# Sums and value products in separate PSUM tiles, output rows by DMAs of 32 partitions, batch edges in the mask, and the second tile's products within the first FFN

## The chip, the cores and the metric

The kernel runs on one core of one Trainium2 chip. The metric is device microseconds of that core, the median of several executions.

## The reference

Sliding-window causal attention (window 64) over 8 batches of 576 rows and 8 heads of 64, followed by a SwiGLU FFN over the 4608 rows that come out:

```
scores = (q @ k^T) / 8, masked to 0 <= i - j < 64
attn   = exp(scores) / sum(exp(scores)) @ v          # 8 x 8 x 576 x 64
x      = attn as 4608 x 512
out    = (silu(x @ w_gate) * (x @ w_val)) @ w_out     # d_ff = 1536, fp32 out
```

## The kernel before

The 4608 rows are cut into 9 tiles of 512 ("tile" in this text means these 512 rows, or a buffer where "PSUM tile" is said). A tile has attention for four pairs of heads (`u`), then 12 FFN steps (`gate_value`, 8 matmuls of 128x512 each), then four output projections of 12 matmuls. From tile 2 on, the attention of a tile is laid between the projections of the tile before. The parts that matter:

```python
def sums(t, u, d_ps):                      # denominators, and their inverse on ScalarE
    for h in range(2):
        nc.tensor.matmul(d_ps[64 * h:64 * h + 64, :], ones[:], E[:, h, :])
    nc.scalar.activation(ld[:], d_ps[:], AF.Ln)
    nc.scalar.activation(r[:], ld[:], AF.Exp, scale=-1.0)

def values(t, u, o_ps):                    # 16 products with V, then the scaling
    ... nc.tensor.matmul(blocks(o_ps[64 * h:64 * h + 64], t, m, m + 1), v..., E...)
    nc.vector.tensor_mul(xT[t][:, u, :], o_ps[:], inverse.pop((t, u))[:])

def products(t, u):                        # tiles 2 to 8
    da = ps_a.tile([P, 2, 512], FP32, name="da_ps", tag="a")
    sums(t, u, da[:, 0])
    values(t, u, da[:, 1])

def project(t, s):                         # 12 matmuls, a copy, one output DMA
    ...
    rows = rows.rearrange("(r e) f -> e r f", e=16)[4 * s:4 * s + 4]   # tiles 2 to 8
    nc.sync.dma_start(rows, os_[:])

# the head (cut): tile 0's scores and sums; load tile 1's Q and K; cast V; load gate and value
# weights; load tile 1's V; shift V on VectorE and do tile 0's values; tile 1's scores and sums
front(0)
... cast_v(0); for s in range(4): weights_gv(384 * s, 384 * s + 384)
load_v(nc.gpsimd, v1[1], 1)
back(0)                                    # shift_v by VectorE, then values(0, 0..3)
front(1)
for m in range(12):
    gate_value(0, m)
back(1)                                    # shift_v by VectorE, then values(1, 0..3)
for m in range(12):
    gate_value(1, m) ...
```

`scores` sets a batch edge to zero in the weights `E` by two GpSimd memsets per head pair. `shift_v` builds a copy of V moved by 64 rows, because even and odd blocks of keys need V at different partitions.

The softmax here doesn't subtract the row's maximum and nothing guards it: scores larger than these inputs give would overflow.

## Time and profile before

| | before |
|---|---|
| median of 3 runs | 391.09 us (390.72 to 391.17) |
| span of the profiled run | 390.2 us |
| first FFN starts (its first weight load) | 39.9 us |
| scores of tile 2 | 89.6 us |
| a steady tile, FFN to FFN | 38.4 us |
| last matmul ends | 379.9 us |

In the profile, PE is TensorE (PEld its weight loads), DVE is VectorE, ACT is ScalarE, POOL is GpSimd and SP is SyncE; a q after the name marks the issuing of a DMA by that engine. PSUM is the memory that matmuls write. A "value group" is the 16 products with V of one head pair. The "head" of the kernel is all before the first FFN, its "tail" all after the last matmul. The profiled run of the kernel before took 391.94 us, 0.8 above the median.

In the timeline, a line holds a start, a duration, an engine, a source line of the kernel, an operation, what it writes and reads, and in brackets the idle time just before it and what ended it. The waits view holds, for an engine and line, what was waited for, the total in us, how often, and the longest.

### The profile page before, as it was taken

How to read it: one execution, taken by the hardware profiler on the slowest of the kernel's cores; microseconds unless marked ns; L12 is line 12 of the kernel's file. 1: busy time of each engine (PE TensorE's matmuls, PEld its weight loads, DVE VectorE, ACT ScalarE, POOL GpSimd, SP SyncE). 2: the span in 40 equal slices, each digit the busy share in tenths (PEclk: the TensorE clock that was granted, in tenths of full speed). 3: DMA queues.
4: the chain of work that ended last, by engine and by line, in shares of the span. 5: the costliest groups of instructions: out<-in, count | busy, mean ns of one | idle time of the engine just before them, and what ended most of it. 6: DMA issues, size and time to landing. Idle time of an engine off the chain costs nothing.

```text
span 390.2 us, 6851 instructions
## 1 busy us (share of the span) xinstructions
PE 333.9 (86%) x2670; PEld 159.3 (41%) x2712; DVE 217.9 (56%) x305; ACT 164.4 (42%) x236; POOL 144.5 (37%) x306
## 2 busy tenths in 40 slices
PE   3564996999889997998799979988998899889990
PEld 2353343444334443444344434444444344434440
DVE  4887246576335773577356736673666376633420
ACT  1636531335333366336533753374337434743300
POOL 6962894470076016551652255435423000000000
PEclk9995799899999999999999999999999999999997
DMA  8999899970489606990798079807961130110012
GB/s 266 167 195 182 127 116 174 183 72 35 135 167 231 119 6 126 181 159 9 129 196 142 12 138 187 134 21 144 188 118 28 57 81 2 31 54 25 2 42 66
DMA packets 76224, 43.35 MB, mean 111 GB/s; under 512 B 56928, under 2 KB 70688, under 8 KB 76192
## 3 DMA queue, kind: packets, MB, share of 16 engines
q0 software_dynamic: 38320, 20.37, 41.0%
q1 hardware_dynamic: 36784, 21.50, 21.1%
q10 hardware_dynamic: 1088, 1.05, 0.8%
q8 instruction: 21, 0.34, 0.4%
q14 instruction: 11, 0.09, 0.1%
HBM read 50.14 MB, written 9.44 MB: 153 GB/s over the span
## 4 chain that ended last, share of the span: by engine, by line
PE 80%; DMA 6%; ACT 4%; POOL 3%; issue 2%; DVE 2%; SPq 0%; DVEq 0%; POOLq 0%
PE v_ps L260 24%; PE g_ps L260 24%; PE o_ps L271 23%; ACT ld L230 4%; PE da_ps L241 3%; DMA wg<-in_moe_w_gate_dram 3%; PE da_ps L228 2%; PE s_ps L203 2%; DMA out_dram<-os__4362 2%; DMA q<-in_q_dram 2%; POOL v L139 1%; POOL q_n L79 1%; POOL k_n L79 1%; POOL wg L151 0%; POOL wv L151 0%
## 5 line engine op out<-in xcount | busy, mean ns | idle before, releaser
L265 ACT ACTIVATE sg<-g_ps 128x512 f32<-128x512 f32 x108 | 64.5, 597 | 134.4 <-PE g_ps L260 109.6
L266 DVE TENSOR_TENSOR hT<-sg,v_ps 128x512 bf16<-128x512 f32 x108 | 74.8, 693 | 74.9 <-PE v_ps L260 73.9
L260 PE MATMUL v_ps<-xT,wv 128*128 128x512 bf16 x426 | 112.0, 384 | 0.4
L260 PE MATMUL g_ps<-xT,wg 128*128 128x512 bf16 x420 | 110.9, 383 | 0.9 <-issue 0.6
L271 PE MATMUL o_ps<-wo,hT 128*128 128x512 bf16 x408 | 96.3, 380 | 1.7 <-issue 0.8
L110 POOL DMA_DIRECT2D k_s<-in_k_dram x124 | 66.3, 540 | 49.2 <-DMA q_s<-in_q_dram 32.7
L260 PEld LDWEIGHTS <-wv 128*128 128x128 bf16 x432 | 42.7, 99 | 52.2 <-issue 2.2
L260 PEld LDWEIGHTS <-wg 128*128 128x128 bf16 x432 | 42.6, 99 | 52.3 <-issue 2.8
L271 PEld LDWEIGHTS <-hT 128*128 128x128 bf16 x432 | 39.7, 98 | 45.1
L212 ACT ACTIVATE E<-s_ps 128x1024 bf16<-128x1024 f32 (+1 forms) x36 | 35.0, 1008 | 18.0 <-PE s_ps L203 17.9
L222 POOL MEMSET E<- 64x64 bf16 x56 | 6.5, 147 | 83.7 <-DVE E L213 83.7
L187 DVE STREAM_TRANSPOSE kT<-k_s 128x512 bf16<-128x512 bf16 x28 | 35.8, 1277 | 0.0
L246 DVE TENSOR_TENSOR xT<-da_ps,r 128x512 bf16<-128x512 f32 x28 | 19.4, 692 | 23.6 <-ACT r L232 13.6
L230 ACT ACTIVATE ld<-da_ps 128x512 f32<-128x512 f32 x28 | 16.7, 598 | 37.1 <-PE da_ps L228 36.0
L92 POOL DMA_DIRECT2D q_s<-in_q_dram x52 | 28.9, 566 | 3.3 <-DMA v<-in_v_dram 2.5
L241 PE MATMUL da_ps<-E,v 128*64 128x64 bf16 x448 | 12.4, 196 | 19.7 <-ACT ld L230 19.7
L241 PEld LDWEIGHTS <-v 128*64 128x64 bf16 x576 | 14.6, 116 | 33.2 <-issue 29.0
L213 DVE TENSOR_TENSOR E<-E,maskp 128x1024 bf16<-128x1024 bf16 x28 | 19.4, 693 | 12.9 <-ACT E L212 12.9
L232 ACT ACTIVATE r<-ld 128x512 f32<-128x512 f32 x36 | 22.7, 631 | 1.1
L203 PE MATMUL s_ps<-qT,kT 64*64 64x128 bf16 (+1 forms) x640 | 15.1, 229 | 8.5 <-DVE kT L173 7.3
L183 DVE STREAM_TRANSPOSE qT<-q_s 128x512 bf16<-128x512 bf16 x28 | 19.7, 704 | 0.0
L139 POOL CAST v<-v_f 128x512 bf16<-128x512 f32 x28 | 16.6, 630 | 7.2 <-PE da_ps L241 6.4
(83 smaller groups left out, 170.7 us busy)
## 6 DMA issues: line engine op xcount, KB each, us to landing
v_f<-in_v_dram SPq DMA_DIRECT2D x25, 256.0 KB
k_s<-in_k_dram POOLq DMA_DIRECT2D x100, 56.0 KB, 5.5
v<-v SPq DMA_DIRECT2D x7, 256.0 KB
wg<-in_moe_w_gate_dram POOLq DMA_DIRECT2D x4, 384.0 KB, 9.2
wv<-in_moe_w_val_dram POOLq DMA_DIRECT2D x4, 384.0 KB, 11.2
wo<-in_moe_w_out_dram POOLq DMA_DIRECT2D x2, 768.0 KB, 9.3
q_s<-in_q_dram POOLq DMA_DIRECT2D x8, 186.0 KB, 6.5
v<-v SPq DMA_DIRECT2D x7, 192.0 KB
```

The source lines that it names most:

```text
L92: nc.gpsimd.dma_start(q_s[p0:p0 + n // 16, :, 0:w], q[b, a:H:2, s0:s0 + n].rearrange("u (r e) d -> r u (e d)", e=16) [:, :, 32 * c:32 * c ...
L110: nc.gpsimd.dma_start(k_s[p0:p0 + m // 4, o // P, :, 0:w], k[b, a:H:2, s:s + m].rearrange("u (r e) d -> r u (e d)", e=4) [:, :, 32 * c:32 ...
L187: nc.vector.transpose(kT[t % 2][:, u, :].rearrange("r (g x e) -> r g e x", g=4, e=4), k_s[:, :, u].rearrange("r g (e d) -> r g e d", d=D)[ ...
L203: nc.tensor.matmul(blocks(s_ps[64 * c:64 * c + 64, h], t, lo, hi), src[r, u, 64 * (j % 8):64 * (j % 8) + 64], blocks(qT[r], t, lo, hi),)
L212: nc.scalar.activation(E[:, :, lo:512], s_ps[:, :, lo:512], AF.Exp, scale=0.125)
L230: nc.scalar.activation(ld[:], d_ps[:], AF.Ln)
L232: nc.scalar.activation(r[:], ld[:], AF.Exp, scale=-1.0)
L241: nc.tensor.matmul(blocks(o_ps[64 * h:64 * h + 64], t, m, m + 1), (v1 if m % 2 else v2)[t % 2][:, m // 2, 2 * u + h, :], blocks(E[:, h, :] ...
L260: nc.tensor.matmul(ps[:], w[:, c, P * m:P * m + P], xT[t][:, c, :], start=(c == 0), stop=(c == 3),)
L265: nc.scalar.activation(sg[:], g_ps[:], AF.Silu)
L266: nc.vector.tensor_mul(hT[t][:, m, :], sg[:], v_ps[:])
L271: nc.tensor.matmul(o_ps[:], hT[t][:, c, P * s:P * s + P], wo[:, c, :], start=(c == 0), stop=(c == 11),)
```

## The change

It has five intents: let the value products start without the logarithm; send the output rows over more DMA engines; take the batch edges out of the attention path by keeping them in the mask; copy Q out of PSUM unbroken, in one run of columns (the first two tiles keep their columns in another order, so that also `blocks` and the mask change); and fill TensorE's gaps in the head by laying tile 0's values between tile 1's scores, and tile 1's values after FFN steps 7 to 10 (counted from 0, so step 7 is the eighth), with V shifted by DMA. The diff, cut to its core:

```diff
     def blocks(ap, t, lo, hi):
-        if t < TURNED:
-            return ap[:, 64 * lo:64 * hi]
-        return ap.rearrange("r (e x) -> r e x", e=16)[:, :, 4 * lo:4 * hi]
+        e = 4 if t < TURNED else 16
+        w = 64 // e
+        return ap.rearrange("r (e x) -> r e x", e=e)[:, :, w * lo:w * hi]
...
-        for i, x in enumerate((queries[t], kT[t % 2])):
-            nc.vector.tensor_copy(
-                x[:, u, :].rearrange("p (r e) -> p e r", e=4),
-                tp[:, i, :].rearrange("p (e r) -> p e r", e=4),
-            )
+        nc.vector.tensor_copy(queries[t][:, u, :], tp[:, 0, :])
+        nc.vector.tensor_copy(
+            kT[t % 2][:, u, :].rearrange("p (r e) -> p e r", e=4),
+            tp[:, 1, :].rearrange("p (e r) -> p e r", e=4),
+        )
...
-        if 0 < t < 8:
-            a = 64 * (1 - t % 2)
-            for h in range(2):
-                nc.gpsimd.memset(blocks(E[a:a + 64, h, :], t, t, t + 1), 0.0)
+    def clear_part(t):
+        nc.gpsimd.memset(part(maskp, t)[0], 0.0)
+    def restore_part(t):
+        ...                                  # two GpSimd copies per tile
...
     def products(t, u):
-        da = ps_a.tile([P, 2, 512], FP32, name="da_ps", tag="a")
-        sums(t, u, da[:, 0])
-        values(t, u, da[:, 1])
+        sums(t, u, ps_f.tile([P, 512], FP32, name="d_ps", tag="v"))
+        values(t, u, ps_a.tile([P, 2, 512], FP32, name="ao_ps", tag="a")[:, 0])
...
-        o_ps = ps_f.tile([P, 512], FP32, name="o_ps", tag="gv"[s % 2])
+        o_ps = ps_f.tile([P, 512], FP32, name="o_ps", tag="g")
...
-            rows = rows.rearrange("(r e) f -> e r f", e=16)[4 * s:4 * s + 4]
-        nc.sync.dma_start(rows, os_[:])
+            for i in range(4):
+                eng = nc.scalar if t == NT - 1 and i % 2 else nc.sync
+                eng.dma_start(
+                    rows.rearrange("(r e) f -> e r f", e=16)[4 * s + i], os_[32 * i:32 * i + 32]
+                )
...
     cast_v(0)
+    shift_v(0, shift_dma)
     for s in range(4):
         weights_gv(384 * s, 384 * s + 384)
     load_v(nc.gpsimd, v1[1], 1)
-    back(0)
-    front(1)
+    shift_v(1, shift_dma)
+    front(1, lambda u: back(0, u))           # values(0, u) between the scores of tile 1
...
     for m in range(12):
         gate_value(0, m)
-    back(1)
+        if 7 <= m < 11:
+            back(1, m - 7)
```

More of the change, by code (lines that the diff above doesn't have):

```diff
@@ L54 @@
     tri = cst.tile([P, 2, 64], BF16, name="tri")
-    mask = cst.tile([P, 2, 4, 2, 64], BF16, name="mask")
+    mask = cst.tile([P, 2, 4, 4, 2, 16], BF16, name="mask")
     maskp = cst.tile([P, 2, 16, 4, 2, 4], BF16, name="maskp")
@@ L207, in scores @@
                 )
+        Ev, sv = [x[:].rearrange("r h (e x) -> r h e x", e=4) for x in (E, s_ps)]
         if t == 0:
-            nc.vector.memset(E[64:128, :, 0:64], 0.0)
-            nc.scalar.activation(E[0:64, :, 0:64], s_ps[0:64, :, 0:64], AF.Exp, scale=0.125)
-        lo = 0 if t else 64
-        nc.scalar.activation(E[:, :, lo:512], s_ps[:, :, lo:512], AF.Exp, scale=0.125)
+            nc.vector.memset(Ev[64:128, :, :, 0:16], 0.0)
+            for h in range(2):
+                nc.scalar.activation(
+                    Ev[0:64, h, :, 0:16], sv[0:64, h, :, 0:16], AF.Exp, scale=0.125
+                )
+                nc.scalar.activation(
+                    Ev[:, h, :, 16:128], sv[:, h, :, 16:128], AF.Exp, scale=0.125
+                )
+        else:
+            nc.scalar.activation(E[:], s_ps[:], AF.Exp, scale=0.125)
         nc.vector.tensor_mul(
@@ L215, in scores, with part @@
             E[:].rearrange("r h x -> r (h x)"),
-            mask[:].rearrange("r h i c x -> r (h i c x)") if t < TURNED
+            mask[:].rearrange("r h e i c x -> r (h e i c x)") if t < TURNED
             else maskp[:].rearrange("r h e i c x -> r (h e i c x)"),
         )
-        if 0 < t < 8:
-            a = 64 * (1 - t % 2)
-            for h in range(2):
-                nc.gpsimd.memset(blocks(E[a:a + 64, h, :], t, t, t + 1), 0.0)
         weights[t, u] = E
+    def part(ap, t):
+        i, c = divmod(t, 2)
+        r = slice(64 - 64 * c, P - 64 * c)
+        return ap[r, :, :, i, c, :], tri[r, c, :]
+    def clear_part(t):
+        nc.gpsimd.memset(part(maskp, t)[0], 0.0)
+    def restore_part(t):
+        dst, src = part(maskp, t)
+        for h in range(2):
+            nc.gpsimd.tensor_copy(dst[:, h], src.rearrange("r (x e) -> r e x", e=16))
     def sums(t, u, d_ps):
@@ L278, in project @@
         if t < TURNED:
-            rows = rows[P * s:P * s + P]
+            nc.sync.dma_start(rows.rearrange("(r e) f -> e r f", e=4)[s], os_[:])
         else:
-            rows = rows.rearrange("(r e) f -> e r f", e=16)[4 * s:4 * s + 4]
-        nc.sync.dma_start(rows, os_[:])
+            for i in range(4):
+                eng = nc.scalar if t == NT - 1 and i % 2 else nc.sync
+                eng.dma_start(
+                    rows.rearrange("(r e) f -> e r f", e=16)[4 * s + i], os_[32 * i:32 * i + 32]
+                )
     def set_exp():
@@ L310, with front @@
         )
-    flat = tri[:].rearrange("r c x -> r (c x)")
-    nc.vector.tensor_copy(
-        mask[:].rearrange("r h i c x -> r (h i) (c x)"),
-        flat.rearrange("r (n x) -> r n x", n=1).broadcast_to([P, 8, P]),
-    )
+    for i in range(4):
+        nc.vector.tensor_copy(
+            mask[:, 0, :, i], tri[:].rearrange("r c (x e) -> r e c x", e=4)
+        )
+    nc.vector.tensor_copy(mask[:, 1], mask[:, 0])
     staged[0] = [cast.tile([P, H, 4, D], BF16, name=n, tag=n) for n in ("q_b", "k_b")]
-    def front(t):
+    def front(t, other=None):
         for u in range(6):
@@ L329, in front, with back, shift_dma @@
                 scores(t, u - 1)
+            if other and 0 < u < 5:
+                other(u - 1)
             if u > 1:
                 sums(t, u - 2, ps_f.tile([P, 512], FP32, name="d_ps", tag="v"))
-    def back(t):
-        shift_v(t, nc.vector.tensor_copy)
-        for u in range(4):
-            values(t, u, ps_a.tile([P, 2, 512], FP32, name="ao_ps", tag="a")[:, 1])
+    def back(t, u):
+        values(t, u, ps_a.tile([P, 2, 512], FP32, name="ao_ps", tag="a")[:, 0])
+    def shift_dma(dst, src):
+        nc.sync.dma_start(dst, src)
     front(0)
+    nc.vector.memset(part(mask, 1)[0], 0.0)
     staged[1] = [
@@ L363 @@
     nc.vector.tensor_copy(maskp[:, 1], maskp[:, 0])
+    clear_part(2)
     load_v(nc.gpsimd, v1[0], 2)
@@ L369 @@
             turn(2, m // 3)
-    def shift_dma(dst, src):
-        nc.sync.dma_start(dst, src)
     shift_v(2, shift_dma)
@@ L395 @@
         if t + 1 < NT:
+            restore_part(t)
+            if t + 1 < 8:
+                clear_part(t + 1)
             cast_v(t + 1)
```

## The prediction

> **What bounds the kernel now.** I read the page's busy shares and chain first. TensorE is busy for 86% of the span, and four fifths of the chain that ended last is TensorE's, nearly all of it the three dense matmul groups of the FFN:
>
> ```profile
> PE 333.9 (86%) x2670; PEld 159.3 (41%) x2712; DVE 217.9 (56%) x305; ACT 164.4 (42%) x236; POOL 144.5 (37%) x306
> ...
> PE 80%; DMA 6%; ACT 4%; POOL 3%; issue 2%; DVE 2%; SPq 0%; DVEq 0%; POOLq 0%
> ```
>
> So there are two ways to be faster: TensorE waiting less between its dense stretches, and a shorter head and tail, where it waits or is done. Dense matmuls follow each other every 0.216 us (four take 0.864 us in the chain in order of time). The FFN of 9 tiles needs 9 x (96 + 48) x 0.216 = 280 us of that; 111 us are other things. The longest waits in total say what:
>
> ```profile
> PE da_ps L241 <- ACT ld L230: 19.7, 28, 0.7
> ```
>
> This is the only large wait of TensorE: 28 times (7 tiles of 4 head pairs), 0.7 us each, the value products wait for the logarithm that ScalarE takes of the sums. The timeline of one pair of head pairs in a steady tile shows it in place:
>
> ```profile
> 222.60 0.41 PE L228 MATMUL da_ps<-E,ones 128*64 128x512 bf16 x2
> ...
> 223.07 0.60 ACT L230 ACTIVATE ld<-da_ps 128x512 f32<-128x512 f32 x1 [1.28 <-PE da_ps L228]
> ...
> 223.72 0.44 PE L241 MATMUL da_ps<-E,v 128*64 128x64 bf16 x16 [0.72 <-ACT ld L230]
> ...
> 223.97 0.41 PE L228 MATMUL da_ps<-E,ones 128*64 128x512 bf16 x2
> ...
> 225.07 0.44 PE L241 MATMUL da_ps<-E,v 128*64 128x64 bf16 x16 [0.69 <-ACT ld L230]
> ```
>
> Sums start at 222.60 and values only at 223.72, when the logarithm has ended; then the next sums follow 0.25 us after the start of the values. The values don't use the logarithm: they write the other half of the tile that it reads.
>
> The timeline of the head and of the gap between the first two FFNs:
>
> ```profile
> 32.31 0.25 POOL L222 MEMSET E<- 64x64 bf16 x2
> 32.53 0.67 PE L228 MATMUL d_ps<-E,ones 128*64 128x512 bf16 x2 [2.02 <-POOL E L222]
> ...
> 63.50 0.55 DVE L146 COPY v<-v 64x1536 bf16<-64x1536 bf16 x1
> 64.09 0.69 DVE L147 COPY v<-v 64x2048 bf16<-64x2048 bf16 x1
> 64.83 0.77 PE L241 MATMUL ao_ps<-E,v 128*64 128x64 bf16 x32 [2.36 <-DVE v L147]
> ```
>
> At 32 us a small GpSimd memset of the batch edge holds TensorE for 2.0 us; GpSimd had been issuing a DMA that itself waited for weights. At 62.5 us the first FFN is over and TensorE waits for VectorE to shift V. Last, the timeline of the tail:
>
> ```profile
> 378.71 0.69 DVE L276 COPY os__4378<-o_ps 128x512 f32<-128x512 f32 x1 [3.27 <-DMA out_dram<-os__4346]
> 379.43 0.54 SPq L282 DMA_DIRECT2D out_dram<-os__4378  x1
> 382.90 0.69 DVE L276 COPY os__4394<-o_ps 128x512 f32<-128x512 f32 x1 [3.50 <-DMA out_dram<-os__4362]
> 383.62 0.54 SPq L282 DMA_DIRECT2D out_dram<-os__4394  x1
> ```
>
> The matmuls end at 379.9 (369.37 + 10.52), the span at 390.2: 10.3 us of copies waiting for output DMAs.
>
> **What the Trainium skill says.** "PSUM — Partial Sum Buffer", PSUM bank collisions: it is by bank and quadrant that engines must be kept apart. The two halves of the old tile are 512 fp32 each, one bank each, so nothing of the chip asks for the 0.7 us wait; it comes from dependencies kept by tile, and a tile of its own removes it. The trace can't tell bank from tile, but shows the wait. "DMA: Bandwidth & Descriptors", Why a DMA increments its semaphore by 16: a DMA is spread over the largest k <= 16 engines that divides the slowest dimension of both sides. The old output side is 4 x 32 x 512, so k = 4. The trace agrees, between the last issue and its landing:
>
> ```profile
> 383.90:387.90 4.00, 0.00 (x0) 0.00 (x0) 0.00 (x0) 0.00 (x0) 0.00 (x0) 0.60 0.23 60
> ```
>
> DMA share 0.23 of 16 engines is 3.7 engines, at 60 GB/s. "TensorE: Matmul & The Clock Gate", What's actually happening: the array runs at half clock after some 3.4 us of idleness. The trace agrees: 0.50 granted from 30 to 40 us, and 0.43 us a matmul just after 67.8 us. "VectorE: DVE Perf Modes", Why PSUM operands drop a tier: a 2-byte PSUM source can still run at two elements a cycle; the strided copies here take 1.31 us, so an unbroken one should take about 0.43 us (estimate: 512 / 2 / 0.96 GHz + 0.16 of fixed time, that being 0.69 less 512 / 0.96 GHz in the fp32 copy).
>
> **The change, part by part.**
>
> 1. *Separate PSUM tiles*, tiles 2 to 8. Values now follow sums at once: sums take 0.22 us of issue in place of 1.12 (222.60 to 223.72). 0.90 x 4 x 7 = 25.2 us. This lies on the path: TensorE has nothing else there. The inverse (0.47 to start, then 0.60 + 0.63 for the logarithm and exponential of each pair, 0.69 for the product) ends about 3.2 us after the last sums; the next FFN comes 3.28 us after them (0.22 + 0.37 + 2.69 of the last projection). It just fits; I allow 1.5 us in all for where it doesn't.
>
> 2. *Head.* The Q copy goes from 1.31 to about 0.43 us, VectorE being the limit of both first tiles (about 3.35 us per head pair in each). Tile 0: 0.43 + 1.33 + 0.11 + 0.69 = 2.56 each; but its exponentials are split by head (1.07 becomes about 1.5), so its last mask product ends near 18.0 in place of 20.07 us. Before, TensorE then did all of tile 0's values up to 24 us, after VectorE's two V shifts (1.4 us). Now tile 1's transposes come at once, near 18.6, and values are laid between them; V is shifted by DMA from 17.3 us. Per head pair 0.43 + 1.33 + 0.72 + 0.69 = 3.17 us on VectorE. From the first Q copy at 19.3: the first K copy ends near 21.3, the second 23.1, three further rounds bring the last to 29.5, its scores, exponential and mask take 2.5, and the first FFN starts near 32.6, before 39.9: 7.3 us. The GpSimd memset with its 2.0 us is in this.
>
> 3. *Tile 1's values within the first FFN.* Before, from the end of the first FFN (62.5) to the scores of tile 2 (89.6): 27.1 us. After: a full-clock FFN stretch (21.0 us in the steady tiles, 195.0 to 216.0) and four value groups of 0.27: 22.1. Saves 5.0 us, the half-clock stretch included.
>
> 4. *Output DMAs.* 32 rows on the slow dimension give k = 16. A DMA of 256 KB took 5.2 to 5.8 us alone; 64 KB per engine at 60 / 3.7 = 16 GB/s is 4.0 us of it, so about 1.5 us is fixed. After: copy 0.2 + 0.69, two issues on each of two queues 1.08, landing 1.5 + 0.3, and 1.4 us that the span ran on after the last landing: 5.2 in place of 10.3 us. Saves 5.1 us.
>
> 5. *Mask edges and projections all in one tag.* 56 memsets of 0.15 us leave GpSimd, two small copies per tile come; neither is on the path. Projection tiles have two buffers and are emptied 0.9 us after they fill, against 2.7 us for the next: no wait.
>
> Sum: 25.2 + 7.3 + 5.0 + 5.1 - 1.5 = 41.1; 391.1 - 41.1 = **350.0 us**.
>
> **The rivals.** (a) *The inverse becomes the wait*: the FFN start waits for the last product of tile t, or values wait for a PSUM buffer. ScalarE does 4 x 1.23 us for four inverses while TensorE's products shrink to about 2 us. For it: the fit above has 0.1 us to spare. Against: 2.7 us of projection lie after each two. If 1 us per tile were lost: 357 us. (b) *V's shift by DMA comes late in the head*: DMA share is 1.42 from 20 to 40 us, and weight DMAs take 9 to 11 us there. Against: the shift is few large packets on another queue, and is wanted only near 22 us, 4.5 us after it is sent. If it lands at 27: 4 to 5 us lost, 354 us. For tile 1, V has landed by 40.5 us (SyncE could then send a shift) and is wanted near 48 us. (c) *The tail is hidden no better*: if 16 DMAs of 64 KB queue at 0.54 us of issue each, or each has its fixed time in turn, 2 to 3 us of the 5.1 are lost: 352.5. (d) *Denser TensorE work lowers the clock*: it is 1.00 in all steady stretches now, also in those 99.5% busy, so I give it little.
>
> **Range and chances.** Part 1 is sure to about 2 us unless (a) holds; the head is the least sure, by 4 us either way; the tail by 2. Together about 5 us, with more on the slow side for (a) and (b): 345 to 356. Two per cent is 7.8 us; part 1 alone is three times that. Chances: faster 0.97, same 0.02, slower 0.01.
>
> **What would show it.** Part 1: no wait of the value products for the logarithm, steady period 34.8 us (38.4 now), no new wait before the FFN's first matmuls. Part 2: first FFN matmul near 32.6 us; a value group waiting for a DMA would be rival (b). Part 3: no gap between the first two FFNs and no half clock there. Part 4: DMA share well over 0.25 in the last microseconds, about 5 us from last matmul to end. A steady period over 35.5 us, or a first FFN after 36 us, would make the prediction wrong.

## The result and the profile after

The kernel after takes 350.63 us in the median of 4 runs (349.65 to 351.55), the kernel before 391.13 us in the same rounds. The ratio is 0.8964, with a 95% interval of 0.8937 to 0.8991. The prediction was 350.0.

The busy shares and the shares of the chain that ended last, in the page of the kernel after:

```profile
PE 329.5 (95%) x2712; PEld 157.9 (45%) x2712; DVE 209.9 (60%) x305; ACT 163.6 (47%) x244; POOL 142.5 (41%) x268
...
PE 85%; DMA 9%; POOL 4%; SPq 0%; DVE 0%; issue 0%
```

TensorE's busy time is nearly the old one, over a span that is 42 us shorter. ScalarE has left the chain. DMA has taken a larger part of it, which the prediction had only as its rival (b). TensorE's waits, all that the view lists (engine, line, what was waited for: us in total, times, longest us):

```profile
PE tp L169 <- POOL q_b L345: 5.3, 2, 5.0
PE d_ps L245 <- DVE E L220: 3.3, 5, 0.9
PE s_ps L203 <- DVE kT L173: 2.1, 4, 0.9
PE ao_ps L258 <- DMA v<-v: 1.7, 1, 1.7
PE ao_ps L258 <- DVE xT L263: 1.1, 3, 0.7
```

The 19.7 us of waiting for the logarithm are gone, and no new wait stands in the steady tiles. Four of the five rows belong to the head; the fourth, for the DMA of V, stands in the first FFN. The timeline of two head pairs, that answer to the two shown of before:

```profile
200.21 0.41 PE L245 MATMUL d_ps<-E,ones 128*64 128x512 bf16 x2
...
200.45 0.42 PE L258 MATMUL ao_ps<-E,v 128*64 128x64 bf16 x16
...
200.66 0.60 ACT L247 ACTIVATE ld<-d_ps 128x512 f32<-128x512 f32 x1 [1.32 <-PE d_ps L245]
...
200.70 0.39 PE L245 MATMUL d_ps<-E,ones 128*64 128x512 bf16 x2
...
200.92 0.42 PE L258 MATMUL ao_ps<-E,v 128*64 128x64 bf16 x16
```

Values now start 0.24 us after the sums, where it was 1.12, while ScalarE reads the sums. The two head pairs, that had filled 2.85 us (222.59 to 225.44), take 1.07 (200.21 to 201.28). At the end of the stage the last scaling comes in time for the FFN:

```profile
206.86 0.69 DVE L263 TENSOR_TENSOR xT<-ao_ps,r 128x512 bf16<-128x512 f32 x1 [0.46 <-ACT r L249]
207.41 0.74 PEld L276 LDWEIGHTS <-wg 128*128 128x128 bf16 x4
207.63 1.03 PE L276 MATMUL g_ps<-xT,wg 128*128 128x512 bf16 x4
```

The scaling ends at 207.55 and the first matmul of the FFN is at 207.63, with no idle time noted. The margin is as thin as the prediction said, and it held in every tile: the steady period is 34.8 us.

The head of the kernel after, in the timeline and in the chain that ended last (start, duration, what):

```profile
30.98 1.64 PE L276 MATMUL g_ps<-xT,wg 128*128 128x512 bf16 x4
...
48.40 0.52 PE L258 MATMUL ao_ps<-E,v 128*64 128x64 bf16 x16 [1.75 <-DMA v<-v]
```

```profile
20.94 11.57 DMA wg<-in_moe_w_gate_dram
...
32.79 9.69 DMA v<-in_v_dram
...
42.53 5.82 DMA v<-v
...
48.40 0.52 PE ao_ps L258 x16
```

The first FFN starts at 31.0 us. After its eighth step TensorE waits 1.75 us for the shifted V of tile 1, and the chain goes back through that shift (5.8 us), through V (9.7 us), to a DMA of gate weights that GpSimd had to see landed before it could issue the last part of V. One round of VectorE in the head, from one K copy of tile 1 to the next (the mask and the scaling, not shown, lie between):

```profile
23.80 0.41 DVE L172 COPY qT<-tp 128x512 bf16<-128x512 bf16 x1
24.13 1.30 DVE L173 COPY kT<-tp 128x512 bf16<-128x512 bf16 x1
...
26.79 1.28 DVE L173 COPY kT<-tp 128x512 bf16<-128x512 bf16 x1
```

The unbroken Q copy takes 0.41 us, where the strided one took 1.31. Last, the tail, in the timeline:

```profile
343.30 0.69 DVE L292 COPY os__4478<-o_ps 128x512 f32<-128x512 f32 x1 [1.90 <-PE o_ps L287]
344.02 0.78 SPq L299 DMA_DIRECT2D out_dram<-os__4478  x2
344.02 0.85 ACTq L299 DMA_DIRECT2D out_dram<-os__4478  x2
```

and the busy view of a stretch just after the last issue began (window, its length, busy time of the five engines, granted clock, DMA share, GB/s):

```profile
344.50:346.00 1.50, 0.00 (x0) 0.00 (x0) 0.00 (x0) 0.00 (x0) 0.00 (x0) 0.77 0.65 175
```

No copy waits for a DMA now, and the DMA share is 0.65 where it was 0.23. The span ends 4.6 us after the last matmul.

By stage, with boundaries read from the two timelines (first weight load of the first FFN, scores of tile 2, last matmul's end; the same boundaries hold for the stage figures of the experiments):

| stage | before | after | saved | predicted |
|---|---|---|---|---|
| head, to the first FFN | 39.9 | 31.0 | 8.9 | 7.3 |
| first two FFNs, to tile 2's scores | 49.7 | 47.0 | 2.7 | 5.0 |
| tiles 2 to 8, to the last matmul | 290.3 | 265.3 | 25.0 | 25.2 |
| tail | 10.3 | 4.6 | 5.7 | 5.1 |
| sum | 390.2 | 347.9 | 42.3 | 42.6, less 1.5 allowed for |

The table compares one run of each kernel, and not runs at the medians: the run of before was 0.8 us above its median, the run of after (349.65 us) the fastest of four, 1.0 us under its median. So the sum is 42.3 us where the medians differ by 40.5.

### The profile page after: what moved, and what is told of

Same layout as the page of the kernel before. It is cut to its first block, busy times and chain, and to the rows that moved or that the text cites. A ratio compares the mean times of both kernels' runs of the same rounds, so it can differ in the third digit from the quotient of the medians.

```text
span 347.9 us, 6990 instructions
## 1 busy us (share of the span) xinstructions
PE 329.5 (95%) x2712; PEld 157.9 (45%) x2712; DVE 209.9 (60%) x305; ACT 163.6 (47%) x244; POOL 142.5 (41%) x268
## 4 chain that ended last, share of the span: by engine, by line
PE 85%; DMA 9%; POOL 4%; SPq 0%; DVE 0%; issue 0%
PE o_ps L287 28%; PE g_ps L276 25%; PE v_ps L276 25%; DMA wg<-in_moe_w_gate_dram 3%; DMA v<-in_v_dram 3%; PE ao_ps L258 2%; PE s_ps L203 2%; PE d_ps L245 2%; DMA v<-v 2%; DMA q<-in_q_dram 2%; POOL v L139 1%; POOL q_n L79 1%; POOL k_n L79 1%; POOL wg L151 0%; POOL wv L151 0%; POOL q_b L345 0%
## 5 line engine op out<-in xcount | busy, mean ns | idle before, releaser
L287 PE MATMUL o_ps<-wo,hT 128*128 128x512 bf16 x432 | 99.0, 380 | 0.0
L276 PEld LDWEIGHTS <-wv 128*128 128x128 bf16 x432 | 42.5, 98 | 51.6 <-issue 1.1
L287 PEld LDWEIGHTS <-hT 128*128 128x128 bf16 x432 | 39.6, 98 | 45.1
L263 DVE TENSOR_TENSOR xT<-ao_ps,r 128x512 bf16<-128x512 f32 x36 | 24.8, 689 | 22.0 <-ACT r L249 20.5
L219 ACT ACTIVATE E<-s_ps 128x1024 bf16<-128x1024 f32 x32 | 31.4, 1021 | 12.8 <-PE s_ps L203 12.7
L247 ACT ACTIVATE ld<-d_ps 128x512 f32<-128x512 f32 x36 | 21.3, 591 | 25.2 <-PE d_ps L245 23.1
L240 POOL COPY maskp<-tri 64x64 bf16<-64x64 bf16 x12 | 3.1, 285 | 69.6 <-DVE E L220 69.6
L139 POOL CAST v<-v_f 128x512 bf16<-128x512 f32 x28 | 17.1, 649 | 6.4 <-DMA v_f<-in_v_dram 6.2
L183 DVE STREAM_TRANSPOSE qT<-q_s 128x512 bf16<-128x512 bf16 x28 | 19.7, 704 | 0.0
L245 PE MATMUL d_ps<-E,ones 128*64 128x512 bf16 x72 | 15.8, 431 | 3.3 <-DVE E L220 3.3
L258 PE MATMUL ao_ps<-E,v 128*64 128x64 bf16 x576 | 15.9, 199 | 3.0 <-DMA v<-v 1.7
## 6 DMA issues: line engine op xcount, KB each, us to landing
wg<-in_moe_w_gate_dram POOLq DMA_DIRECT2D x4, 384.0 KB, 10.3
```

The costliest lines, as they stand in the source:

```text
L219: nc.scalar.activation(E[:], s_ps[:], AF.Exp, scale=0.125)
L276: nc.tensor.matmul(ps[:], w[:, c, P * m:P * m + P], xT[t][:, c, :], start=(c == 0), stop=(c == 3),)
L287: nc.tensor.matmul(o_ps[:], hT[t][:, c, P * s:P * s + P], wo[:, c, :], start=(c == 0), stop=(c == 11),)
```

## The experiments

The table's third row agrees and the first two err in opposite senses. So the questions were: is each part worth what its stage shows, alone and undone; what sets the pace of the head; and is a place within the FFN what tile 1's values gain from?

E1 to E4, E5 to E8 and E9 to E12 ran on three chips, with the kernel before at 391.51, 391.65 and 391.15 us in their rounds. E1 to E4 are set against the 350.63 us of other rounds; when the kernel after was run again (E5) its median was 1.0 us higher, so these differences are sure to about 1 us.

### E1: undo the separate PSUM tiles

```diff
-        sums(t, u, ps_f.tile([P, 512], FP32, name="d_ps", tag="v"))
-        values(t, u, ps_a.tile([P, 2, 512], FP32, name="ao_ps", tag="a")[:, 0])
+        da = ps_a.tile([P, 2, 512], FP32, name="da_ps", tag="a")
+        sums(t, u, da[:, 0])
+        values(t, u, da[:, 1])
```

> The kernel after, with the sums and the value products of tiles 2 to 8 again in the two halves of one PSUM tile; all else as after. Theory (the wait for the logarithm is on the path, 0.90 us x 28): +25.2 us on 350.6, so 375.8 us, the wait of the value products for the logarithm back at some 0.7 us x 28, steady period 38.4 us. Rival (something else in the change made the attention stage shorter, or the wait would be hidden by now): clearly under +20 us.

Measured: 374.94 us (ratio to before 0.9574), 24.3 us over the kernel after. Tiles 2 to 8 take 24.7 us longer, the steady period is 38.3 us, and the old wait is back, as the waits view of this run shows:

```profile
PE da_ps L258 <- ACT ld L247: 19.3, 28, 0.7
```

The theory holds.

### E9: the separate PSUM tiles alone, in the kernel before

The same two lines the other way round, and the projections in one tag (PSUM tiles of one tag take turns in its two buffers).

> The kernel before with one part alone: sums and value products in separate PSUM tiles (and the projections in one tag, which frees the buffers for it). Theory (the wait of 0.90 us x 28 and nothing else, independent of the other parts): -25 us on 391.4, so 366.4 us; steady period 34.8 us. Rival (with the old output DMAs of 5.2 to 5.8 us the shorter attention stage waits for the output buffers): steady period over 35 us, over 368 us.

Measured: 367.01 us against 391.15 (ratio 0.9384, interval 0.9362 to 0.9406), so 24.1 us. The steady period is 34.8 us and the tail stays at 10.4. Within the scatter the part is worth the same with the others and without them: 24.3 and 24.1 us, by stage 24.7 and 25.0. The output buffers did not become a wait although the old DMAs are slow.

### E2: undo the output DMAs of 32 partitions

```diff
-            for i in range(4):
-                eng = nc.scalar if t == NT - 1 and i % 2 else nc.sync
-                eng.dma_start(...[4 * s + i], os_[32 * i:32 * i + 32])
+            rows = rows.rearrange("(r e) f -> e r f", e=16)[4 * s:4 * s + 4]
+            nc.sync.dma_start(rows, os_[:])
```

> The kernel after, with each output block of tiles 2 to 8 again one DMA of 128 partitions on SyncE's queue. Theory (4 of 16 engines, a cost in the tail alone): the tail from the last matmul to the end goes from 4.6 back to 10.3 us, steady period stays 34.8 us, so +5.7 us, 356.3. Rival 1 (the shorter attention stage now waits for the output buffers too): steady period over 35 us, total over 358. Rival 2 (the split is worth little): under +3 us.

Measured: 358.29 us (355.78 to 358.64; ratio to before 0.9133), 7.7 us over the kernel after in the medians, 2 us more than expected. In its profile the tail is 10.8 us (after: 4.6) and the steady period 34.8 us, so rival 1 falls. The rest of it lies in the first two FFNs, where this run waited 3.2 us for tile 1's shifted V. The unchanged kernel shows the same scatter (E5), so E2 alone doesn't size this part well.

### E10: the output DMAs alone, in the kernel before

> The kernel before with one part alone: output rows of tiles 2 to 8 by four DMAs of 32 partitions. Theory (a cost of the tail alone): tail 4.6 us in place of 10.3, the rest unchanged: -5.7 us, 385.7 us. Rival: if undoing this in the kernel after cost 7.7 us because the DMAs also get in the way elsewhere, -7 or more.

Measured: 386.08 us against 391.15 (ratio 0.9877, interval 0.9858 to 0.9897), so 5.1 us in the medians. The tail is 4.4 us, and the steady period is unchanged at 38.4. It is a cost of the tail alone, and the surplus of E2 is not this part's. One thing is untested: in the last tile the DMAs are not only of 32 partitions but also shared by two queues, and E2 and E10 change both together. In a steady tile four issues take SyncE's queue 1.73 us (from 201.04 in the profile after), in the tail two on each queue take 0.8; so the second queue may be some 0.9 us of the gain (an estimate from these two records).

### E3: undo the batch edges in the mask

```diff
+        if 0 < t < 8:
+            a = 64 * (1 - t % 2)
+            for h in range(2):
+                nc.gpsimd.memset(blocks(E[a:a + 64, h, :], t, t, t + 1), 0.0)
```

and the calls of `clear_part` and `restore_part`, with the clearing in the first mask, are taken out.

> The kernel after, with the batch edges again set to zero by two GpSimd memsets per head pair (and the mask left alone). Theory: GpSimd reaches the memsets of tile 1 only when it has issued its weight and value DMAs (31.7 us in the profile after), so the sums of tile 1, wanted from 24.3 us on, hold TensorE until 32 us; the first FFN starts near 38 us in place of 31.0; the wait of 1.75 us for the shifted values goes in exchange: total +5 to +7 us, 356 to 357.5. Rival A (what the prediction had: the memset is worth its 2.0 us): +2. Rival B (off the path): 0. Steady period unchanged in all.

Measured: 357.22 us (ratio 0.9121), 6.6 us over the kernel after. The timeline of this run:

```profile
33.10 0.88 POOL L127 DMA_DIRECT2D v<-in_v_dram  x1 [1.06 <-DMA wg<-in_moe_w_gate_dram]
33.97 0.43 POOL L229 MEMSET E<- 64x64 bf16 x4
34.19 0.67 PE L249 MATMUL d_ps<-E,ones 128*64 128x512 bf16 x2 [9.36 <-POOL E L229]
```

A memset of some 0.1 us stands on GpSimd behind DMA issues that wait for weight DMAs to land, and TensorE stands behind it for 9.4 us. The first FFN starts at 41.1 us, 10.1 us later (expected 7), of which the missing wait for V and what follows it give back 2.1; between the two profiled runs it is 7.6 us. The prediction had put this part down as off the path but for the 2.0 us that the old head showed. With the head pulled forward it would have cost most of what the head gains: the mask is what makes the rest of the head possible.

### E4: the unbroken Q copy done three times

```diff
-        nc.vector.tensor_copy(queries[t][:, u, :], tp[:, 0, :])
+        for _ in range(3):
+            nc.vector.tensor_copy(queries[t][:, u, :], tp[:, 0, :])
```

> The kernel after, with the unbroken copy of Q out of PSUM (0.42 us, 8 of them) done three times in place, so that it costs VectorE 1.26 us as the strided one did (1.31). Theory (VectorE sets the pace of the first two tiles): up to 8 x 0.84 = 6.7 us later start of the first FFN, less the 1.75 us wait for the shifted values at its eighth step, which starts at a fixed time: +4 to +5 us, 355. Rival (the pace is set by the chain of scores, exponential and mask, VectorE has room): under +2 us.

Measured: 354.25 us (ratio 0.9045), 3.6 us over the kernel after. The first FFN starts at 37.4 us, 6.5 us later, nearly the full 6.7 of the eight copies. In the waits view of this run TensorE waits for the K copies, which follow the Q copies on VectorE, 7.2 us in place of 2.1:

```profile
PE s_ps L204 <- DVE kT L174: 7.2, 7, 1.8
```

So VectorE does set the pace of the head. But the two FFNs then take 44.7 us in place of 47.0: the wait for tile 1's V is gone, and 2.3 us come back. So part of what the head gains is paid again after the eighth step of the FFN, because V comes at its own time.

### E5: the kernel after again

> The kernel after, unchanged, as the measure for the three below on the same chip. All theories: 350.6 us within 1 us, one wait of 1 to 3 us for the DMA-shifted values of tile 1.

Measured: 351.63 us (349.63 to 352.63; ratio 0.8969), in the rounds of E6 to E8. Its profile waited longer than the first one:

```profile
PE ao_ps L258 <- DMA v<-v: 3.8, 2, 3.3
```

That is 3.3 us after the eighth step and 0.4 us for tile 0's shift, just outside what was expected, as the time is. The two FFNs took 49.3 us, 2.3 more than in the first profile of the same kernel. The wait for this DMA scatters from run to run.

The same holds for tile 0's shift, in the head. In the eight profiles with this head and V issued as here (the kernel after, E1, E2, E4 to E8), TensorE waits for it 0 to 1.7 us, and without E4 the first FFN starts at 30.7 to 32.2 us. The profile that the stage table rests on, with no such wait and a start at 31.0, is one of the better ones.

### E6: the value groups one step later

```diff
-        if 7 <= m < 11:
-            back(1, m - 7)
+        if 8 <= m:
+            back(1, m - 8)
```

> The kernel after with tile 1's four value groups one step later in the first FFN (steps 8 to 11 in place of 7 to 10). Theory (the shifted V lands at about 48.4 us, whatever TensorE does, and the wait of 1.75 us for it is on the path): the wait goes, the last group now stands right before the second FFN and costs some 0.4 us, so -1.3 us against the kernel after on the same chip. Rival (the wait is hidden, the second FFN is held by something else): 0.

Measured: 348.93 us (ratio 0.8908), 2.7 us under E5, more than the 1.3 expected, since E5 had waited 3.3 us and not 1.75. No value group of tile 1 waits any more (tile 0's first still waits 1.4 us); the two FFNs take 45.1 us. The wait is on the path.

### E7: the value groups two at a time

```diff
-        if 7 <= m < 11:
-            back(1, m - 7)
+        if 9 <= m < 11:
+            back(1, 2 * m - 18)
+            back(1, 2 * m - 17)
```

> The kernel after with tile 1's value groups two at a time, after steps 9 and 10. Theory: the wait of 1.75 us goes, and each change between dense matmuls and values costs some 0.2 us of the 0.47 us by which a step with a value group is longer, so two changes less are 0.4 to 0.5 us: -2.2 us against the kernel after on the same chip. Rival (a second group waits for VectorE, which lies between): -1.5 or less.

Measured: 347.71 us (346.27 to 349.50; ratio 0.8877, interval 0.8851 to 0.8903), 3.9 us under E5. Two groups and the return to dense matmuls, in the timeline of this run:

```profile
50.14 0.70 PE L258 MATMUL ao_ps<-E,v 128*64 128x64 bf16 x32
50.77 1.04 PE L276 MATMUL g_ps<-xT,wg 128*128 128x512 bf16 x3
```

From one step's first matmul to the next's it is 2.46 us here (50.77 to 53.23) against 1.73 us without values, so two groups cost 0.73 us; in the kernel after one group lengthens its step by 0.47 us (51.05 to 53.25). The two FFNs take 44.3 us, 0.8 less than E6. Of the shifts only tile 0's is waited for here, 1.0 us.

### E8: the value groups after the first FFN

```diff
         gate_value(0, m)
-        if 7 <= m < 11:
-            back(1, m - 7)
+    for u in range(4):
+        back(1, u)
```

> The kernel after with tile 1's four value groups after the first FFN, as in the kernel before, but with V still shifted by DMA. Theory of the prediction's third step (being within the FFN is what is worth some 2 to 5 us: no gap, no half clock): slower than the kernel after by 2 us or more. Rival (the gap was the late shift on VectorE, not the place of the value groups): the groups take 2.3 us together as they did before (64.83 to 67.10 us), in place of the 1.75 us of wait and 4 x 0.47 us now, so -1.3 us.

Measured: 348.23 us (347.82 to 348.56; ratio 0.8889), 3.4 us **under** E5. The timeline between the two FFNs:

```profile
53.01 0.69 PE L258 MATMUL ao_ps<-E,v 128*64 128x64 bf16 x32
54.53 0.44 PE L258 MATMUL ao_ps<-E,v 128*64 128x64 bf16 x16 [0.82 <-DVE xT L263]
55.12 0.44 PE L258 MATMUL ao_ps<-E,v 128*64 128x64 bf16 x16 [0.15 <-DVE xT L263]
55.50 1.25 PE L276 MATMUL g_ps<-xT,wg 128*128 128x512 bf16 x3
```

Four groups in 2.5 us, and the granted clock stays at 1.00. The old place costs less than the new place with its wait, so the rival holds: the gap of the kernel before was the V shift that VectorE began only after the FFN, not the place of the value groups. Whether a place within the FFN is worth anything once V is there is not shown: E7 does better than E8 by 0.5 us in the medians and E6 worse by 0.7, both within the intervals.

### E11 and E12: tile 1's V issued between the weights

```diff
     for s in range(4):
         weights_gv(384 * s, 384 * s + 384)
-    load_v(nc.gpsimd, v1[1], 1)
+        if s == 1:
+            load_v(nc.gpsimd, v1[1], 1)
```

> The kernel after with one move: GpSimd issues tile 1's V after the second of the four pairs of weight DMAs, not after the last. Theory (the shift waits for V, V waits for its place behind the weights): the shifted V lands several us earlier, the wait before the first value group (1.2 to 3.4 us in three runs) goes, 348 to 349 us, ratio to before 0.889 to 0.891. Rival 1 (the last weights, now later, hold the seventh or tenth step of the first FFN): 351 or more, with a wait of the FFN for a weight DMA. Rival 2 (the shift lands late because the DMA engines are full, not because V comes late): still a wait of over 1 us.

Measured for E11: 347.60 us (347.18 to 350.12; ratio 0.8897, interval 0.8871 to 0.8923). No value group of tile 1 waits any more, and no FFN step waits for weights. The last piece of the shifts was issued by 34.9 us (by 43.7 in the kernel after), and the first value group of tile 1 was wanted only at 48.95, so the margin is wide even though the FFN began later in this run. So V's place behind the weights in GpSimd's queue was the cause of that wait, and both rivals fall. The profiled run was the slowest of the five, and has its wait elsewhere, at the first value group of tile 0:

```profile
PE ao_ps L258 <- DMA v<-v: 2.8, 1, 2.8
```

E12 adds two groups at a time, after steps 8 and 9.

> The version that should beat both: V early as in the run before this one, and tile 1's value groups two at a time after steps 8 and 9. Theory: no wait, and two changes between dense matmuls and values less: 347.5 us, ratio to before 0.887 or less, and less spread from run to run than the kernel after (349.6 to 352.6).

Measured for E12: 349.40 us (348.34 to 350.26; ratio 0.8932, interval 0.8909 to 0.8955). It misses what was expected, and is slower than E7 without the V move. In its profile tile 0's first value group waits 3.3 us for tile 0's shift: the shift was sent at 19.0 us (17.1 in the kernel after), since all of GpSimd's early work came 2 us later in this run, and the group could start 6.9 us after it was sent. From the send to the group it was 4.5 us in the kernel after, 5.4 in E7, 6.4 in E6, 6.7 in E8 and 7.8 in E11. That the V load, now issued 3.4 us after that shift, lengthens it would fit E11, but E12 is hardly above E8, where V was issued late, and these are single profiles of a wait that scatters anyway. It stays open.

## Why the prediction was right, and where it was off

**The total** of 350.0 was met (350.63), in part by luck: by stage the head gave 1.6 us more than predicted and the first two FFNs 2.3 less, and the allowance of 1.5 us was not needed.

**Part 1, separate PSUM tiles**, 25.2 us less an allowance: right in mechanism and size. 25.0 us by stage, 24.3 undone (E1), 24.1 alone (E9). A PSUM tile of its own removes the wait; that the dependency is one kept by tile, and nothing that the chip asks for, stays argued. No late inverse showed; the scaling ended 0.08 us before the matmul that reads it.

**Part 2, the head**, 7.3 us: 8.9. That VectorE sets the pace is shown by E4, which starts the first FFN 6.5 us later for 6.7 us of copies; the copy itself took 0.41 us for the 0.43 estimated. Of the 1.6 us that the first FFN came before its 32.6, 1.4 stand at the end of the last K copy (28.07 for 29.5): 0.9 of it at the end of the second already (22.23 for 23.1), 0.5 in the last round. There the prediction added four durations to 3.17 us, but VectorE went from one K copy of tile 1 to the next in 2.66 us (24.13 to 26.79), with no idle time and each instruction starting 0.07 to 0.20 us before the record of the one before it ends. (The "three further rounds" are two in its own sum: 23.1 + 2 x 3.17 = 29.4.) The step that says that the memset's worth is 2.0 us was wrong in kind: E3 lost 6.6 us. E3 and E4 overlap, so they don't add up to the 8.9; what the other parts of the head are worth (tile 0's values between scores, its V by DMA, the exponentials by head) was not tested alone.

**Part 3, tile 1's values**, 5.0 us: 2.7. Two terms failed. A value group was taken at 0.27 us; it lengthens its step by 0.47 (51.05 to 53.25 is 2.20 against 1.73 us), 0.8 us in all. And the step "V has landed by 40.5 us (SyncE could then send a shift) and is wanted near 48 us" left 7.5 us for a shift that took 5.8, but took the landing from the old profile: V landed at 42.5, 2.0 us later, and with the FFN earlier the shifted V was wanted at 46.6, and there at 48.4. So rival (b) came true, for tile 1, with 1.75 us in this run and 3.3 in E5, and in a small way for tile 0 (up to 1.7 us in E8). E8 shows moreover that the reason given was wrong: with the groups after the FFN, as before, the two FFNs take 44.4 us, less than the 47.0 of the kernel after. The gain over the 49.7 of before comes from the shift that no longer waits for VectorE, and the place within the FFN, as chosen, takes some of it away. The prediction also says that the trace agrees with a half clock after some 3.4 us of idleness. The half clock is there, the idleness is not: the gap before 64.83 us was 2.36 us long, and when the clock fell near 29.7 us no idle stretch of TensorE in the 3.4 us before was over 0.92 us. What brings it on is not shown by these runs.

**Part 4, output DMAs**, 5.1 us: 5.7 by stage, 5.1 alone (E10). Right; the issue of two DMAs on a queue took 0.8 us and not 1.08.

**Rivals (a), (c) and (d)** did not come true: no wait before the FFNs, a tail of 4.6 us, and a clock of 1.00 in all steady stretches at a TensorE share of 95%.

The experiments point to a version that beats both kernels: E7, at 0.8877 of before, where the kernel after had 0.8969 in the same rounds. E6, E8 and E11 are not told apart from it by their intervals.

## What to carry to other kernels

When two products that don't need each other share one PSUM tile, look for the second one waiting for the reader of the first. If no other work lies there, what a second tile is worth is the time from the start of the first product to the start of the second, less what it would be without the wait, times the count: here 0.90 us x 28, more than the 19.7 us that the waits view lists. When a stage is pulled forward, list what it takes from DMAs and from queues with other work in front, each with its time to landing: these don't move with it, and take back the gain at the next point where they are wanted. And before a tiny operation is called off the path, see which engine's queue it stands in and what stands ahead of it.

## What the Trainium skill lacked or had wrong

- "DMA: Bandwidth & Descriptors", Rules for kernel authors, in the row on two transfers to disjoint partition halves, says not to bother and to use one transfer of 128 partitions, as both halves spread over all 16 engines anyway. Here four DMAs of 32 partitions beat one of 128: a tail of 4.4 in place of 10.3 us (E10), DMA share 0.65 in place of 0.23, since the DRAM side of the one has 4 as its slowest dimension. That row lacks the condition, but the table has it in the row on using all 16 engines, so the two must be read together.
- "VectorE: DVE Perf Modes", Terms, under DRAIN, says that the next operation can't issue until the pipe is empty. The records overlap all the same: the Q copy of 0.41 us at 23.80 is followed by the K copy at 24.13, so here durations can't be added up to a pace (3.1 us of durations, 2.66 us of pace per round). The page's section The DRAIN you can't avoid says less flatly that a next op that is not held starts earlier.
- No page that I read says how long a DMA from SBUF to SBUF takes while weights stream in: the V shifts, 64 to 256 KB each, took 5.6 to 6.1 us in the median in the kernel after, beside other transfers.
